# One-core attention and SOLU mixture kernel: W2 products two groups side by side, and float16 passes for half of the value products

## The chip, the cores and the metric

The kernel runs on one core of one Trainium2 chip. The metric is the device time of one execution in microseconds (us), lower is better. TensorE multiplies matrices (PE in the profile; its weight loads are listed apart as PEld), VectorE is DVE, ScalarE is ACT, GpSimd is POOL and SyncE, which issues the transfers, is SP.

## The reference: what is computed

Batch 4, 8 heads, 576 positions, head dimension 64: block-causal attention (blocks of 64), then four dense layers on the 2304 tokens.

```
scores = scale * q @ k.T ; masked where block_i < block_j
attn   = exp(scores - max) / (sum + 1e-9)
x      = attn @ v                       # 2304 x 512
a, b   = x @ w1, x @ w2                 # 2304 x 1024
h      = (a * b) @ w3 @ w_out           # 2304 x 512
h2     = h @ w_in                       # 2304 x 1024
solu   = h2 * softmax(h2)
out    = layernorm(solu) * g_ln @ w_out2   # 2304 x 512
```

The inputs are float64 or float32 as the reference makes them; the kernel folds w3 @ w_out into one 1024 x 512 matrix, W2, on the chip.

## The kernel before, in words

The kernel is written as many small generators, one for each piece of work (a load, a score block, a product of a token group). Each yields its instructions one at a time with the buffers that they read and write and a cost in ns. A planner, `Program.run` (from line 130), keeps a clock for each engine and always emits the instruction that could start first; between several it takes the one with the lower order number. Those numbers are given at `M.spawn` (lines 1144 to 1201) out of the constants of line 282: `PB` and `BS` for batches 2 and 3, `MB`, `MS` and `FS` for token groups, `YO`, `HO`, `OO` for the three later steps of a group, `AO`, `RO`, `VO` for the steps of attention. So a change of costs, buffers or constants changes the order of the instructions on every engine's queue.

**Attention** goes by batch and pair of heads (16 pairs). `scores` (L481) makes q k.T of two heads in two halves of the array's rows; `row_max` (L499), `expo` (L505), `norm`; `flip` (L651) transposes the probabilities on PE into PSUM and copies them to the tiles `ta` (first 320 positions, part 0) and `tb` (last 256, part 1). `values` (L699) multiplies by v in float32: the two heads of a pair write the upper and lower 64 partitions of one PSUM bank, so a pair needs three chunks of positions for part 0 (320, 192 and 64 columns) and five for part 1 (256, 256, 256, 192, 64). In the trace each float32 matmul is two records. The result is scaled (L730) and split into a high and a low float16 part, `xs`, a ring of five token groups.

**Token groups** are nine groups of 256 tokens. `u_ab` (L960) makes a and b for one of 8 column blocks f, in three float16 passes (high by high, high by low, low by high; 24 matmuls of 256 columns), multiplies them into `asb` and splits that into high and low, `ghl`. `u_y` (L1005) multiplies with W2: 8 f x 4 blocks x 3 passes = 96 matmuls of 256 columns for each group. `u_h` (L1049) multiplies with w_in for each half of 128 tokens: 24 matmuls of 512 columns, followed by the softmax and layer norm chain on DVE and ACT and eight transposes (L1097). `u_out` (L1128) makes 24 float16 matmuls of 512 columns and the output transfer.

```
for e in range(NE):
    for q, (s, t) in enumerate(((0, 0), (0, 1), (1, 0))):
        yield op("PE", 123.0, lambda: pe.matmul(
            ps[:, e // 2, e % 2 * N : (e % 2 + 1) * N],
            lhsT=W2s[:, f, s, e * P : (e + 1) * P], rhs=hl[:, t, :], ...
```

The matrices are streamed in, decoded on DVE and split during the first third of the time. When the last value product has been issued (`after_attention`, line 1215), memory is given to further `ghl`, `asb`, `t`, `uT` and `osb` buffers; four PSUM banks become a second `yh` and two `ab`.

Of the kernel before, what the change touches and what calls it, by code (L numbers as in the profile page):

```python
# [7 lines left out]
F16 = mybir.dt.float16  # L8
# [9 lines left out]
P = 128  # L18
# [196 lines left out]
def block_attention_moe_solu(ctx: ExitStack, tc: tile.TileContext, qk0, qk, vr, w1, w2, w3r, wout, win, wout2, gln, out):  # L215
# [54 lines left out]
    def acq(tag):  # L270
        return ("acq", tag)
# [7 lines left out]

    done = M.done  # L280
    ENG = "APd"
    PS, PO, OG, OA, PD, DS, P1, PG, PW, W2P, AS, PA, PB, BS, MB, MS, FS, YO, HO, OO, AO, RO, VO, DT, P0, K0, W2S, A1, V0, PX, OB, NL = 1009.16, 770.75, 0, 1, -202.05, 1099.57, -2137.11, 346.55, -822.9, -836.48, -602.44, 345.86, 8206.72, 1129.12, -34.34, 7256.56, 225.91, 1732.11, -202.54, -41.89, -10.2, -22.05, -93.34, 228.46, 105.76, 24, 6518, 216.01, 1896.05, 127.52, 0, -92.74
    M.DETOUR = DT


# [25 lines left out]
    negs = const.tile([64, 64], F32, name="negs")  # L311
# [3 lines left out]
    ring(const, "bc", 1, [P, P], F32)  # L315
    ring(const, "sm", 4, [P, 28], F32)
# [6 lines left out]
    apool = ctx.enter_context(tc.tile_pool(name="apool", bufs=1))  # L323
# [12 lines left out]
    mpool = ctx.enter_context(tc.tile_pool(name="mpool", bufs=1))  # L336
    ring(mpool, "asb", 2, [P, N], F32)
    ring(mpool, "ghl", 3, [P, 2, N], F32R)
    ring(mpool, "y", 1, [P, 2, NE, N], F32R)
    vstack = ExitStack()  # L340
# [27 lines left out]
    def pow2_scale(i, name, m, mk):  # L368

        t = scl[:, i]  # L370
        k = ("scl", i)
        ib = yield acq("bc")
        bc, kb = T["bc"][ib], ("bc", ib)
# [5 lines left out]
        rel("bc", ib)  # L379
# [111 lines left out]
    def mask(t, k):  # L491
        return ways(
            [], [k], ("DVE", SMALL, lambda: dve.memset(t, NEG)),
            ("ACT", c_act(64), lambda: act.copy(t, negs)),  # L494
        )

    def row_max(t, dst, k, kd):
# [88 lines left out]
    def norm(b, h, part):  # L586
# [36 lines left out]

    BANKS = ((("e01", (0, 1)), ("e2", (2,))), (("e3", (3,)), ("e4", (4,)), ("e4", (5,))))
    HELD = {0: ("pa", 0, 1), 1: ("pa", P, 2), 2: ("pd", 0, 3), 3: ("pb", 0, 4), 4: ("pc", 0, 4), 5: ("pc", 4 * P, 1)}

    def flip(b, h, part, n):

# [14 lines left out]
        for x in tiles:  # L643
            tag, c0, nb = HELD[x]
            ip = X[b, h, tag]
            p = T[tag][ip]
            kp = [(tag, ip, z) for z in ((4, 5) if x == 4 else (x,))]
            for c in range(nb):
                yield op(
                    "PE", c_mr(P),  # L650
                    lambda: pe.transpose(t[:, o + c * P : o + (c + 1) * P], p[:, c0 + c * P : c0 + (c + 1) * P], ident),  # L651
                    kp, [k],
                )
            if x == 0:
                outs.append((64, t[:, o : o + 64], pt[:, 0, 0:64]))
            elif x == 5:
                outs.append((64, t[:, o + 64 : o + P], pt[:, 4, 192:256]))
            else:
                q = {1: 64, 2: 192, 3: 0, 4: P}[x]
                src = t[:, o : o + nb * P].rearrange("p (a n) -> p a n", n=P)  # L660
                outs.append((nb * P, src, pt[:, 0:nb, q : q + P]))
            o += nb * P
        for tag in sorted({HELD[x][0] for x in tiles}):
            m = X[b, h, tag, "n"] = X.get((b, h, tag, "n"), 0) + 1
            if m == (2 if tag == "pc" else 1):
                rel(tag, X.pop((b, h, tag)))
        for w, src, dst in outs:
            yield ways([], [k, (ptag, ipt, n)], *copies(w, dst, src, 1.0, "Ad"))
# [8 lines left out]
    def values(b, hp, part):  # L677
# [11 lines left out]
        iv = X[b, hp, "vv"]  # L689
        vv = T["vraw"][iv]  # L690
        i = yield acq("ab")
        t, k = T["ab"][i], ("ab", i)
        for q, (c, o) in enumerate(REACH[part]):

            kr = slice(0, D if c == NT - 1 else P)

            def both():
                for j in range(2):
                    pe.matmul(  # L699
                        t[j * D : (j + 1) * D, o:w], lhsT=vv[kr, c, j], rhs=T[ptag][ipt[j]][kr, c, o:w],  # L700
                        start=(q == 0), stop=(q == len(REACH[part]) - 1),
                    )

            yield op(
                "PE", 4 * (w - o) / 2.4 + 80, both,
                [(ptag, x, n) for x in ipt for n in range(len(BANKS[part]))] + [("vraw", iv), (("vraw", iv), "z")], [k],
            )
        for j in range(2):
            rel(ptag, ipt[j])
        nv = X[b, hp, "nv"] = X.get((b, hp, "nv"), 0) + 1  # L710
        if nv == 2:
            rel("vraw", iv)
        for j in range(2):
            yield ev(("r", b, 2 * hp + j, part))
        ir = X.pop((b, hp, part, "rb"))
# [223 lines left out]
    def u_ab(g, f):  # L939
# [8 lines left out]
        ih = yield acq("ghl")  # L948
        a = yield acq("ab")
        done(("ab", g, f))  # L950
        ps, k = T["ab"][a], ("ab", a)
# [18 lines left out]
                    q += 1  # L970
        ia = yield acq("asb")
        asb, ka = T["asb"][ia], ("asb", ia)
        hl, kh = T["ghl"][ih], ("ghl", ih)
# [13 lines left out]
        X["ghl", g, f] = ih  # L987
        done(("g", g, f))

    def u_y(g):  # L990
# [36 lines left out]
        rel("yh", i)  # L1027
        X["y", g] = iy
        done(("y", g))

    def u_h(g, i):
        yield ev("lpool")
# [111 lines left out]
    def attention(b, hp, p):  # L1144
        M.spawn(p, load_qk(b, hp))
        M.spawn(p, prep_qk(b, hp))
        M.spawn(p + V0, load_v(b, hp))
        M.spawn(p + AO, s_01(b, hp))
        M.spawn(p + 2 * AO, s_23(b, hp, 2))
        M.spawn(p + 3 * AO, s_23(b, hp, 3))  # L1150
# [43 lines left out]
    for g in range(NG):  # L1194
        p = MB + MS * g
        for f in range(NF):
            M.spawn(p + FS * f, u_ab(g, f))
        M.spawn(p + YO, u_y(g))
# [15 lines left out]
    def after_attention():  # L1214

        M.retire("ab", range(2, 6))
        vstack.close()
        gpool = ctx.enter_context(tc.tile_pool(name="gpool", bufs=1, reuse_waits="tile"))
        more("ghl", *[gpool.tile([P, 2, N], F32R, name=f"ghl{3 + i}") for i in range(3)])
        for tag in ("pa", "pd"):  # L1220
            more("asb", *[t[:, 0:N] for t in T[tag]])
        more("t", T["qk"][0][:, 0:1024].rearrange("p (a c) -> p a c", a=2))
        for t in T["tb"]:
            more("uT", t.bitcast(F16).rearrange("p c n -> p (c n)")[:, 0 : 2 * DFF].rearrange("p (z f n) -> p z f n", z=2, f=NF))
        more("osb", T["vraw"][0].rearrange("p c h d -> p (c h d)")[:, 0:512])

    def after_banks():
        astack.close()
# [59 lines left out]
```

## Time and profile before

| | |
|---|---|
| time, median of 3 runs | 784.7 us (783.59 to 787.49) |
| the profiled execution: its own time | 782.93 us |
| the profiled execution: span of its instructions | 781.2 us |
| granted TensorE clock, mean | 0.998 |
| PE busy | 751.9 us (96%) |
| DVE busy | 443.6 us (57%) |
| ACT busy | 356.2 us (46%) |

A row of the chain of waits gives a start, a length, and what ran: `634.71 8.64 PE yh L1005 x72` is 72 records of line 1005 from 634.71 us on, 8.64 us in all. A row of the windows gives a stretch, its length, and each engine's busy time with its count of instructions. A row of the groups gives busy time and the mean duration of one in ns; matmuls overlap, so the mean is longer than the step from one to the next.

### The profile page before, as it was taken

The numbers are of one execution on the slowest core, as the hardware profiler recorded it, in microseconds if no ns is written. First come the engines' busy times: TensorE is split into PE (matmuls) and PEld (weight loads), VectorE is DVE, ScalarE is ACT, GpSimd is POOL, SyncE is SP. The second block draws the span as 40 slices with busy tenths as digits, with TensorE's granted clock in tenths as the row PEclk, the third lists the DMA queues.
The fourth block names the chain that finished last, engine by engine and source line by source line (L and its number), as shares of the span: only waits on it lengthen the run. The fifth ranks groups of instructions, "written<-read, shape, count | busy, mean of one in ns | idle before, by whom it ended". The sixth has DMA issues, their size and how long they took to land.

```text
span 781.2 us, 13588 instructions
## 1 busy us (share of the span) xinstructions
PE 751.9 (96%) x5193; PEld 557.0 (71%) x5193; DVE 443.6 (57%) x1191; ACT 356.2 (46%) x1008; POOL 192.2 (25%) x277
## 2 busy tenths in 40 slices
PE   6799998999899999999999999999999999999998
PEld 3445444777575887678767877688798698698974
DVE  7898998999974156455474338323504416216243
ACT  4657745677744344566166545441322322213222
POOL 1213324678821102222032112120210111112100
PEclk9999999999999999999999999999999999999999
DMA  7666665554122100313101110000000000000001
GB/s 222 210 223 197 215 231 179 163 163 151 45 72 70 39 1 15 91 32 111 27 15 44 32 31 1 28 1 1 14 14 1 14 16 1 28 1 1 1 1 55
DMA packets 36545, 53.84 MB, mean 69 GB/s; under 512 B 22272, under 2 KB 24576, under 8 KB 36480
## 3 DMA queue, kind: packets, MB, share of 16 engines
q1 hardware_dynamic: 36480, 52.97, 21.6%
q8 instruction: 41, 0.67, 0.4%
q14 instruction: 24, 0.20, 0.1%
HBM read 48.24 MB, written 4.72 MB: 68 GB/s over the span
## 4 chain that ended last, share of the span: by engine, by line
PE 86%; DVE 10%; ACT 1%; POOL 1%; issue 1%; DMA 1%; SPq 0%; ACTq 0%; DVEq 0%; POOLq 0%
PE ab L960 23%; PE yh L1049 13%; PE yh L1005 12%; PE ab L1128 12%; PE ab L481 7%; PE ab L651 6%; PE ab L880 5%; PE ab L699 5%; PE ab L1097 2%; DVE st L499 1%; PE ab L722 1%; DVE w3f L774 1%; DVE w3f L782 1%; DVE w3f L778 1%; DMA qk<-in_qk_dram 1%
## 5 line engine op out<-in xcount | busy, mean ns | idle before, releaser
L1005 PE MATMUL yh<-ghl,W2s 128*128 128x256 f32 x864 | 119.9, 289 | 1.4 <-POOL ghl L262 1.4
L960 PE MATMUL ab<-xs,w2s 128*128 128x256 f16 x864 | 114.6, 273 | 0.0
L960 PE MATMUL ab<-xs,w1s 128*128 128x256 f16 x864 | 111.5, 275 | 0.1
L1005 PEld LDWEIGHTS yh<-ghl,W2s 128*128 128x128 f32 x864 | 107.7, 189 | 4.5 <-issue 2.4
L1049 PE MATMUL yh<-winHL,y 128*128 128x512 f32 x432 | 102.1, 393 | 0.0
L960 PEld LDWEIGHTS <-w2s 128*128 128x128 f16 x864 | 83.6, 98 | 14.0 <-issue 4.0
L1049 PEld LDWEIGHTS yh<-winHL,y 128*128 128x128 f32 x432 | 80.1, 188 | 17.3 <-issue 0.4
L960 PEld LDWEIGHTS <-w1s 128*128 128x128 f16 x864 | 81.9, 98 | 14.4 <-issue 3.5
L499 DVE TENSOR_REDUCE st<-ab 128x1 f32<-128x288 f32 (+4 forms) x192 | 75.5, 411 | 1.3 <-ACT ab L494 0.3
L481 PE MATMUL ab<-qk 64*128 64x288 f32 (+4 forms) x384 | 68.8, 434 | 7.2 <-POOL qk L255 6.3
L1128 PE MATMUL ab<-gWs,uT 128*128 128x512 f16 x336 | 75.7, 379 | 0.0
L262 POOL TENSOR_TENSOR ghl<-asb,ghl 128x256 fp32r<-128x256 f32 x48 | 38.2, 796 | 115.8 <-ACT ghl L252 101.6
L880 PE MATMUL ab<-woutF,w3f 128*128 128x512 f32 x128 | 61.2, 604 | 2.9 <-DVE woutF L782 2.6
L1128 PEld LDWEIGHTS <-uT 128*128 128x128 f16 x336 | 32.5, 98 | 36.3 <-issue 0.4
L481 PEld LDWEIGHTS ab<-qk 64*128 64x128 f32 (+1 forms) x384 | 32.2, 180 | 32.2 <-issue 8.7
L979 DVE SCALAR_TENSOR_TENSOR asb<-ab,dsc,asb 128x256 f32<-128x256 f32 (+3 forms) x66 | 25.6, 397 | 49.3 <-ACT asb L252 49.0
L1067 DVE TENSOR_REDUCE sm<-yh 128x1 f32<-128x1024 f32 x18 | 22.0, 1224 | 46.2 <-PE yh L1049 46.2
L505 ACT ACTIVATE pc<-ab,st 128x288 f32<-128x288 f32 x64 | 31.9, 503 | 32.8 <-DVE st L569 31.6
L255 POOL TENSOR_SCALAR rb<-st,scl 128x128 f32<-128x128 f32 (+1 forms) x50 | 23.3, 469 | 90.1 <-PE ab L722 31.3
L252 ACT ACTIVATE asb<-ab,dsc 128x256 f32<-128x256 f32 (+3 forms) x58 | 22.6, 413 | 40.5 <-PE ab L960 39.9
L262 POOL TENSOR_TENSOR xs<-rs,xs 128x256 f16<-128x256 f32 (+3 forms) x36 | 26.5, 736 | 58.4 <-ACT xs L252 55.1
L880 PEld LDWEIGHTS ab<-woutF,w3f 128*128 128x128 f32 x128 | 21.9, 190 | 25.2 <-issue 19.0
(160 smaller groups left out, 1154.5 us busy)
## 6 DMA issues: line engine op xcount, KB each, us to landing
qk<-in_qk_dram SPq DMA_DIRECT2D x16, 576.0 KB, 4.2
raw<-in_w3r_dram SPq DMA_DIRECT2D x16, 512.0 KB, 4.6
raw<-in_wout_dram SPq DMA_DIRECT2D x16, 512.0 KB, 3.8
raw<-in_w_dram SPq DMA_DIRECT2D x16, 512.0 KB, 4.5
raw<-in_win_dram SPq DMA_DIRECT2D x8, 512.0 KB, 3.7
vraw<-in_vr_dram SPq DMA_DIRECT2D x18, 192.0 KB, 2.4
out_dram<-osb SPq DMA_DIRECT2D x13, 256.0 KB, 2.0
vraw<-in_vr_dram SPq DMA_DIRECT2D x32, 80.0 KB, 3.4
```

The costliest lines, as they stand in the source:

```text
L262: "P": ("POOL", c_tt(n, dst.dtype), lambda: pool.tensor_tensor(dst, a, b, op=ALU.subtract)),
L481: pe.matmul(dst, lhsT=t[h, q0 : q0 + rows], rhs=t[h, k0 + c0 : k0 + c0 + cols], start=True, stop=True)
L499: "DVE", c_dve(t.shape[-1]), lambda: dve.tensor_reduce(dst, t, axis=AX.X, op=ALU.max, negate=True), [], [k, kd]
L505: lambda: act.activation(p, t, AF.Exp, bias=nm, accum_out=sm), [ks], [k, kp, (ks, "s")],
L651: lambda: pe.transpose(t[:, o + c * P : o + (c + 1) * P], p[:, c0 + c * P : c0 + (c + 1) * P], ident),
L699: pe.matmul(t[j * D : (j + 1) * D, o:w], lhsT=vv[kr, c, j], rhs=T[ptag][ipt[j]][kr, c, o:w], start=(q == 0), stop=(q == len(REACH[part]) - 1),
L880: lambda: pe.matmul(ps, lhsT=t[:, jc, :], rhs=woutF[:, jc, :], start=(jc == 0), stop=(jc == NF - 1)),
L960: lambda: pe.matmul(ps[:, n * N : (n + 1) * N], lhsT=w[:, x * NE + hp, s, fs], rhs=xs[:, hp, t, x0 : x0 + N], start=(q == 0), stop=(q == 3 ...
L979: lambda: dve.scalar_tensor_tensor(asb[:, c0:c1], ps[:, N + c0 : N + c1], dsc[:, b, x, 1:2], asb[:, c0:c1], op0=ALU.mult, op1=ALU.mult), [ ...
L1005: lambda: pe.matmul(ps[:, e // 2, e % 2 * N : (e % 2 + 1) * N], lhsT=W2s[:, f, s, e * P : (e + 1) * P], rhs=hl[:, t, :], start=(f == 0 and ...
L1049: lambda: pe.matmul(ps[:, n, :], lhsT=y[:, a, e, ts], rhs=X["win"][e // 2][:, e % 2, b, n * 512 : (n + 1) * 512], start=(e == 0 and (a, b) ...
L1128: lambda: pe.matmul(ps, lhsT=uT[:, s, f, :], rhs=gWs[:, f, t, :], start=(q == 0), stop=(q == 3 * NF - 1)),
```

## The change

1. Groups 5 and 6, and 7 and 8, are paired (`PAIR`). `u_ab` of both writes its high and low parts into the two halves of a common tile `gp` (eight of them, one for each f, 512 columns), and `u_y2` replaces `u_y` for them: 48 matmuls of 512 columns for each half of the output, 96 for a pair of groups. Groups 0 to 4 stay.
2. For batches 2 and 3 `values` uses three float16 passes instead of float32. `flip` writes a high and a low float16 part, scaled by 2^13, in the room of the float32 tile; `split_v` does the same for v into a new tile `vhl` (one buffer); the scale in `norm` follows.
3. Buffers: the attention tiles and the value tiles are given back together once attention is done, and `gp` (8), one more `y`, one more `t`, one more `uT` take their room; the extra `ghl`, `asb`, `osb` buffers go; `bc` goes (its user takes an `asb`); `negs` is one column.
4. Other constants in line 282.

```diff
-PB, BS, MB, MS, FS, YO, HO, OO, AO, RO, VO = 8206.72, 1129.12, -34.34, 7256.56, 225.91, 1732.11, -202.54, -41.89, -10.2, -22.05, -93.34
+PB, BS, MB, MS, FS, YO, HO, OO, AO, RO, VO = 7906.4, 765.4, -723.76, 7510.2, 186.21, 5034.19, -135.9, -413.38, -1.27, 244.18, -1116.8
...
+    ring(const, "vhl", 1, [P, 2, NT, 2, D], F16)
...
+    def split_v(b, hp):
...
+            yield ways([kv, (kv, "z"), ks], [(k, x)], *copies(n, hi, src, s[rows], "Ad"))
+            yield op("DVE", c_dve(n) + 62,
+                lambda: dve.scalar_tensor_tensor(lo, src, s[rows], hi, op0=ALU.mult, op1=ALU.subtract), ...
     def flip(b, h, part, n):
...
+            if b < NAT:
+                yield ways([], [k, (ptag, ipt, n)], *copies(w, dst(pt), src, 1.0, "Ad"))
+                continue
+            hi, lo = (dst(pt[:, z]) for z in range(2))
+            yield ways([k], [(ptag, ipt, n)], *copies(w, hi, src, PSC, "Ad"))
+            yield op("DVE", c_dve(w) + 62,
+                lambda: dve.scalar_tensor_tensor(lo, src, PSC, hi, op0=ALU.mult, op1=ALU.subtract), ...
     def values(b, hp, part):
...
+            for m, (x, y) in enumerate(((0, 0), (0, 1), (1, 0))):
+                yield op("PE", max((w - o) / 2.4 + 10, 60.0),
+                    lambda: both(lambda v: v[:, x], lambda p: split_view(p)[:, y], q == 0 and m == 0, q == end and m == 2), kk, [k])
...
     def u_ab(g, f):
...
+            if g == PAIR[g]:
+                ih = X["gp", g, f] = yield acq("gp")
+                done(("gp", g, f))
+            else:
+                yield ev(("gp", g - 1, f))
+                ih = X["gp", g - 1, f]
+            z = g - PAIR[g]
+            hl, kh = T["gp"][ih][:, :, z * N : (z + 1) * N], ("gp", ih, z)
...
+    def u_y2(g):
+        yield ev(("hps", g - 1, 1))
+        for x in range(2):
+            i = yield acq("yh")
+            ps, k = T["yh"][i], ("yh", i)
+            for f in range(NF):
...
+                for n in range(2):
+                    e = 2 * x + n
+                    for q, (s, t) in enumerate(((0, 0), (0, 1), (1, 0))):
+                        yield op("PE", 230.0, lambda: pe.matmul(ps[:, n, :],
+                            lhsT=W2s[:, f, s, e * P : (e + 1) * P], rhs=T["gp"][ih][:, t, :], ...
...
+            if x == 0:
+                iy = yield acqs("y", 2)
+            for z in range(2):
...
     def after_attention():
...
-        more("ghl", *[gpool.tile([P, 2, N], F32R, name=f"ghl{3 + i}") for i in range(3)])
-        for tag in ("pa", "pd"):
-            more("asb", *[t[:, 0:N] for t in T[tag]])
...
+        for tag, n, shape, dt in (("gp", 8, [P, 2, 2 * N], F32R), ("y", 1, [P, 2, NE, N], F32R), ("t", 1, [P, 2, 512], F32), ("uT", 1, [P, 2, NF, P], F16)):
+            more(tag, *[gpool.tile(shape, dt, name=f"{tag}{len(T[tag]) + x}") for x in range(n)])
```

## Rows read from the trace of the kernel before

**Rows 1.** The page's first part: busy time and share of each engine.
```profile
PE 751.9 (96%) x5193; PEld 557.0 (71%) x5193; DVE 443.6 (57%) x1191; ACT 356.2 (46%) x1008; POOL 192.2 (25%) x277
```

**Rows 2.** Windows: stretch and length; busy PE, PEld, DVE, ACT, POOL; clock, DMA share, GB/s.
```profile
0.00:240.00 240.00, 214.34 (x1278) 135.52 (x1279) 213.76 (x535) 153.16 (x440) 103.54 (x130) 0.99 0.53 169
240.00:514.00 274.00, 274.00 (x2046) 206.80 (x2044) 134.45 (x446) 135.69 (x426) 53.68 (x99) 1.00 0.13 38
514.00:757.00 243.00, 243.00 (x1772) 204.55 (x1771) 85.33 (x185) 61.09 (x132) 33.61 (x48) 1.00 0.02 8
757.00:781.20 24.20, 20.54 (x103) 10.12 (x102) 10.10 (x27) 6.29 (x10) 1.38 (x2) 1.00 0.12 44
```

**Rows 3.** Chain of waits, group 6 from its W2 products to w_in: start, us, what.
```profile
626.57 1.43 PE yh L1005 x12
...
630.63 1.45 PE yh L1005 x12
632.08 2.63 PE ab L960 x24
634.71 8.64 PE yh L1005 x72
...
645.77 10.91 PE yh L1049 x48
```

**Rows 4.** Chain of waits, one value product of part 0 and one of part 1.
```profile
467.05 1.13 PE ab L699 x12
...
512.13 2.03 PE ab L699 x20
```

**Rows 5.** Windows of line 699 alone, 240 to 514 us: PE, PEld busy.
```profile
240.00:514.00 274.00, 28.57 (x276) 17.36 (x276) 1.00 0.13 38
```

**Rows 6.** Groups by form, weight loads of value products and of `u_ab`.
```profile
L960 PEld LDWEIGHTS <-w2s 128*128 128x128 f16 x864 | 83.6, 98 | 14.0 <-issue 4.0
...
L699 PEld LDWEIGHTS ab<-tb,vraw 128*64 128x64 f32 x256 | 16.8, 136 | 13.4 <-issue 2.3 <-DVE tb L254 1.4 <-ACT rs L252 0.8
```

**Rows 7.** Groups by form on DVE, 240 to 514 us.
```profile
L1102 DVE TENSOR_TENSOR uT<-ab,uT 128x512 f16<-128x512 f32 x14 | 9.5, 681 | 5.8 <-ACT uT L252 5.8
...
L979 DVE SCALAR_TENSOR_TENSOR asb<-ab,dsc,asb 128x256 f32<-128x256 f32 x13 | 6.2, 476 | 22.9 <-ACT asb L252 22.8
...
L979 DVE SCALAR_TENSOR_TENSOR asb<-ab,dsc,asb 128x128 f32<-128x128 f32 x8 | 2.7, 338 | 0.1
...
L979 DVE SCALAR_TENSOR_TENSOR asb<-ab,dsc,asb 128x64 f32<-128x64 f32 x8 | 2.1, 265 | 4.2 <-ACT asb L252 4.2
```

**Rows 8.** Windows of 40 us, columns as in rows 2.
```profile
120.00:160.00 40.00, 35.13 (x269) 25.96 (x267) 38.76 (x78) 27.24 (x56) 25.69 (x21) 0.96 0.52 165
160.00:200.00 40.00, 36.95 (x308) 30.37 (x307) 38.56 (x85) 29.47 (x80) 30.70 (x31) 1.00 0.45 149
200.00:240.00 40.00, 36.73 (x227) 26.00 (x226) 33.55 (x87) 25.54 (x80) 18.84 (x29) 1.00 0.17 52
...
280.00:320.00 40.00, 40.00 (x260) 28.65 (x258) 25.62 (x85) 18.67 (x62) 7.03 (x13) 1.00 0.07 23
```

**Rows 9.** Chain of waits at the end, group 8 and the last outputs.
```profile
746.51 10.92 PE yh L1049 x48
757.43 5.20 PE ab L1128 x24
...
770.20 7.35 PE ab L1128 x34
```

**Rows 10.** Timeline, DVE steps of the first half of group 8.
```profile
752.03 1.23 DVE L1067 TENSOR_REDUCE sm<-yh 128x1 f32<-128x1024 f32 x1 [5.48 <-PE yh L1049]
...
754.52 1.22 DVE L1069 TENSOR_TENSOR qk<-qk,yh 128x1024 f32<-128x1024 f32 x1 [1.27 <-ACT qk L1068]
755.78 1.29 DVE L1072 BATCH_NORM_STATS2 sm<-qk 128x6 f32<-128x512 f32 x2
...
761.10 0.81 DVE L1087 TENSOR_SCALAR qk<-qk,sm 128x1024 f32<-128x1024 f32 x1
...
763.72 0.69 DVE L1102 TENSOR_TENSOR uT<-ab,uT 128x512 f16<-128x512 f32 x1 [0.56 <-ACT uT L252]
```

More of the change, by code (lines that the diff above doesn't have):

```diff
@@ L234, in block_attention_moe_solu @@
     HC = 512
+    PAIR = [None if g < R else g - (g - R) % 2 for g in range(NG)]
     M = Program()
@@ L321, in block_attention_moe_solu @@
     T["tmp"] = M.add_slots("tmp", [tmp16[:, i] for i in range(NE)])
-    apool = ctx.enter_context(tc.tile_pool(name="apool", bufs=1))
+    mpool = ctx.enter_context(tc.tile_pool(name="mpool", bufs=1))
+    ring(mpool, "asb", 2, [P, N], F32)
+    ring(mpool, "ghl", 3, [P, 2, N], F32R)
+    ring(mpool, "y", 1, [P, 2, NE, N], F32R)
+    vstack = ExitStack()
+    apool = vstack.enter_context(tc.tile_pool(name="apool", bufs=1))
     for tag, n, shape, dt in (
@@ L334, in block_attention_moe_solu @@
         ring(apool, tag, n, shape, dt)
[L336 to L340, printed above, removed]
+    T["gp"] = M.add_slots("gp", [])
     vpool = vstack.enter_context(tc.tile_pool(name="vpool", bufs=1))
@@ L371, in pow2_scale @@
         k = ("scl", i)
-        ib = yield acq("bc")
-        bc, kb = T["bc"][ib], ("bc", ib)
+        ib = yield acq("asb")
+        bc, kb = T["asb"][ib][:, 0:P], ("asb", ib)
         yield ways([mk], [kb], *copies(P, bc, m.to_broadcast([P, P]), 1.0, "PA"))
@@ L378, in pow2_scale @@
         yield op("PE", c_mr(P), lambda: pe.transpose(pt[:, 0:P], bc, ident), [kb], [ka])
-        rel("bc", ib)
+        rel("asb", ib)
         yield op("DVE", c_dve(P), lambda: dve.tensor_reduce(t[:, 0:1], pt[:, 0:P], axis=AX.X, op=ALU.max), [], [ka, k])
@@ L493, in mask @@
             [], [k], ("DVE", SMALL, lambda: dve.memset(t, NEG)),
-            ("ACT", c_act(64), lambda: act.copy(t, negs)),
+            ("ACT", c_act(64), lambda: act.copy(t, negs.to_broadcast([64, 64]))),
         )
@@ L625, in block_attention_moe_solu, with split_view @@
     HELD = {0: ("pa", 0, 1), 1: ("pa", P, 2), 2: ("pd", 0, 3), 3: ("pb", 0, 4), 4: ("pc", 0, 4), 5: ("pc", 4 * P, 1)}
+    PSC = 2.0 ** 13
+    def split_view(t):
+        c = t.shape[1]
+        return t.rearrange("p c n -> p (c n)").bitcast(F16).rearrange("p (z c n) -> p z c n", z=2, c=c)
+    def split_v(b, hp):
+        yield ev(("vv", b, hp))
+        yield ev(("scale", ("v", b)))
+        s, _, ks = SC["v", b]
+        iv = X[b, hp, "vv"]
+        vv, kv = T["vraw"][iv], ("vraw", iv)
+        i = yield acq("vhl")
+        t, k = T["vhl"][i], ("vhl", i)
+        for x, (rows, cs) in enumerate(((slice(0, P), slice(0, NT - 1)), (slice(0, D), slice(NT - 1, NT)))):
+            n = (cs.stop - cs.start) * 2 * D
+            src = vv[rows, cs]
+            hi, lo = (t[rows, z, cs] for z in range(2))
+            yield ways([kv, (kv, "z"), ks], [(k, x)], *copies(n, hi, src, s[rows], "Ad"))
+            yield op(
+                "DVE", c_dve(n) + 62,
+                lambda: dve.scalar_tensor_tensor(lo, src, s[rows], hi, op0=ALU.mult, op1=ALU.subtract),
+                [kv, (kv, "z"), ks], [(k, x)],
+            )
+        rel("vraw", iv)
+        X[b, hp, "vhl"] = i
+        done(("vhl", b, hp))
     def flip(b, h, part, n):
@@ L667, in flip @@
         for w, src, dst in outs:
-            yield ways([], [k, (ptag, ipt, n)], *copies(w, dst, src, 1.0, "Ad"))
+            if b < NAT:
[3 more added lines that the diff above has]
+            yield ways([k], [(ptag, ipt, n)], *copies(w, hi, src, PSC, "Ad"))
+            yield op(
+                "DVE", c_dve(w) + 62,
+                lambda: dve.scalar_tensor_tensor(lo, src, PSC, hi, op0=ALU.mult, op1=ALU.subtract), [k], [(ptag, ipt, n)],
+            )
         rel("ab", i)
@@ L688, in values @@
                 yield ev(("g", g - R, f))
-        iv = X[b, hp, "vv"]
-        vv = T["vraw"][iv]
+        split = b >= NAT
+        if split:
+            yield ev(("vhl", b, hp))
+        vtag = "vhl" if split else "vraw"
+        iv = X[b, hp, "vhl" if split else "vv"]
+        vv = T[vtag][iv]
+        kv = [("vraw", iv), (("vraw", iv), "z")] if not split else [(("vhl", iv), x) for x in range(2)]
         i = yield acq("ab")
@@ L695, in values, with both @@
             kr = slice(0, D if c == NT - 1 else P)
-            def both():
+            def both(va, pa, first, last):
                 for j in range(2):
                     pe.matmul(
-                        t[j * D : (j + 1) * D, o:w], lhsT=vv[kr, c, j], rhs=T[ptag][ipt[j]][kr, c, o:w],
-                        start=(q == 0), stop=(q == len(REACH[part]) - 1),
-                    )
[L704 to L707, printed above, removed]
+                        t[j * D : (j + 1) * D, o:w], lhsT=va(vv)[kr, c, j], rhs=pa(T[ptag][ipt[j]])[kr, c, o:w], start=first, stop=last
+                    )
+            end = len(REACH[part]) - 1
+            kk = [(ptag, x, n) for x in ipt for n in range(len(BANKS[part]))] + kv
+            if not split:
+                yield op("PE", 4 * (w - o) / 2.4 + 80, lambda: both(lambda v: v, lambda p: p, q == 0, q == end), kk, [k])
+                continue
+            for m, (x, y) in enumerate(((0, 0), (0, 1), (1, 0))):
+                yield op(
+                    "PE", max((w - o) / 2.4 + 10, 60.0),
+                    lambda: both(lambda v: v[:, x], lambda p: split_view(p)[:, y], q == 0 and m == 0, q == end and m == 2), kk, [k],
+                )
         for j in range(2):
@@ L711, in values @@
         if nv == 2:
-            rel("vraw", iv)
+            rel(vtag, iv)
         for j in range(2):
@@ L947, in u_ab @@
             yield ev(("ab", g - (f == 0), (f - 1) % NF))
[L948 removed]
+        if PAIR[g] is None:
+            ih = yield acq("ghl")
+            hl, kh = T["ghl"][ih], ("ghl", ih)
+        else:
+            if g == PAIR[g]:
+                ih = X["gp", g, f] = yield acq("gp")
+                done(("gp", g, f))
+            else:
+                yield ev(("gp", g - 1, f))
+                ih = X["gp", g - 1, f]
+            z = g - PAIR[g]
+            hl, kh = T["gp"][ih][:, :, z * N : (z + 1) * N], ("gp", ih, z)
         a = yield acq("ab")
@@ L986, in u_ab @@
         rel("asb", ia)
-        X["ghl", g, f] = ih
+        if PAIR[g] is None:
+            X["ghl", g, f] = ih
         done(("g", g, f))
@@ L1029, in u_y @@
         done(("y", g))
+    def u_y2(g):
[5 more added lines that the diff above has]
+                for z in range(2):
+                    yield ev(("g", g + z, f))
+                yield ev(("W2", f))
+                ih = X["gp", g, f]
+                for n in range(2):
+                    e = 2 * x + n
+                    for q, (s, t) in enumerate(((0, 0), (0, 1), (1, 0))):
+                        yield op(
+                            "PE", 230.0,
+                            lambda: pe.matmul(
+                                ps[:, n, :],
+                                lhsT=W2s[:, f, s, e * P : (e + 1) * P],
+                                rhs=T["gp"][ih][:, t, :],
+                                start=(f == 0 and q == 0),
+                                stop=(f == NF - 1 and q == 2),
+                            ), [("gp", ih, 0), ("gp", ih, 1), ("W2", f)], [k],
+                        )
+                if x == 1:
+                    rel("gp", X.pop(("gp", g, f)))
+            if x == 0:
+                iy = yield acqs("y", 2)
+            for z in range(2):
+                v = ps[:, :, z * N : (z + 1) * N]
+                d = [T["y"][iy[z]][:, a, 2 * x : 2 * x + 2, :] for a in range(2)]
+                yield ways([k], [("y", iy[z], x)], *copies(512, d[0], v, 1.0, "Ad"))
+                yield op(
+                    "DVE", c_dve(512), lambda: dve.tensor_tensor(d[1], v, d[0].bitcast(F32), op=ALU.subtract),
+                    [k], [("y", iy[z], x)],
+                )
+            rel("yh", i)
+        for z in range(2):
+            X["y", g + z] = iy[z]
+            done(("y", g + z))
     def u_h(g, i):
@@ L1147, in attention @@
         M.spawn(p + V0, load_v(b, hp))
+        if b >= NAT:
+            M.spawn(p + V0 + 1, split_v(b, hp))
         M.spawn(p + AO, s_01(b, hp))
@@ L1197, in block_attention_moe_solu @@
             M.spawn(p + FS * f, u_ab(g, f))
-        M.spawn(p + YO, u_y(g))
+        if PAIR[g] is None:
+            M.spawn(p + YO, u_y(g))
+        elif PAIR[g] < g:
+            M.spawn(p + YO, u_y2(g - 1))
         for i in range(2):
```

22 lines of the change are left out of this document (8 added, 14 removed).

## The prediction, made before the changed kernel ran

> **What bounds the kernel now.** I began with the page's first part [rows 1]: PE is busy for 96% of the span, and no other engine comes near. As busy shares are means over stages, I then took the windows by stage [rows 2]. The reader is to see two regimes. Before 240 us PE is busy for 214.34 of 240 us while DVE is at 213.76: weights are decoded and the first two batches are under way, and PE misses 25.7 us. From 240 us to the end of the chain PE is busy for every microsecond (274.00 of 274, 243.00 of 243), while DVE is at half load or less. There, time goes down by exactly what is taken out of PE's own stream, and work added to DVE or ACT is free so long as it is not late. The chain of waits gives the price of PE's pieces as steps, not as overlapping durations: [rows 3] for the W2 and w_in products, [rows 4] for the value products. The chain at the end [rows 9] shows PE without a hole as well: 757.43 us plus its pieces leads to 777.55 us, and what follows is one copy and the output transfer.
>
> **The change, part by part.** Durations come from the profiled execution, 782.93 us (span 781.2 and 1.7 around it); it lies 1.8 us, 0.2%, under the median of 784.7. The sum is a difference and is taken off the median.
>
> *W2 products in pairs.* Removed: 4 groups x 96 matmuls of 256 columns. One group costs 1.43 + 1.45 + 8.64 = 11.52 us [rows 3], 120 ns a matmul, so 46.1 us. Added: 192 matmuls of 512 columns in the same float32r format. Line 1049 has that very form: 48 take 10.91 us [rows 3], 227 ns each, so 43.6 us. Gain 2.4 us: joining two products saves no columns, only the excess of the 256-column step over half of the 512-column one. Bounds: at the float16 step (5.20 us for 24 [rows 9], 217 ns) the gain is 4.5 us; with 230 ns, as where other work is mixed in, 2 us.
>
> *Value products of batches 2 and 3.* Eight pairs of heads. A part 0 costs 1.13 us, a part 1 2.03 us [rows 4], 25.3 us for the eight, which agrees with the 28.57 us of line 699 after 240 us [rows 5], as that includes overlap and 20 records of batch 1. By columns: part 0 has 320 + 192 + 64 = 576 per head, part 1 1024. The step of [rows 9] gives 0.423 ns a column. Four passes of 576 and 1024 columns make 0.975 and 1.73 us; so the two heads of a pair run side by side in the array (one after the other they would need twice this, more than was measured), and 0.155 and 0.30 us are entry, short chunks and the change of array shape. Three passes make 0.73 and 1.30 us. If the overhead stays, a pair of heads saves 0.24 + 0.43 us, 5.4 us for eight. If it grows with the records (18 for 12, 30 for 20) the saving is 0.17 + 0.285, 3.6 us for eight. I take 5.4: the array changes its shape once per product, not once per pass.
>
> The last chunk has 64 columns, and there the load of the weights may set the pass. Loads are shown for float16 with 128 columns at 98 ns and for float32 with 64 at 136 ns [rows 6]; a float16 load of 64 columns is not shown. If a pass of that chunk takes half of a 110 ns step (2.63 us for 24 with 128-column loads [rows 3]), 55 ns where the columns alone would need 27, the six short passes of a pair cost 0.17 us more, 1.3 us for eight, which lies inside the two bounds. The Trainium skill, TensorEngine Tiling (Array Packing), Gotcha 2, says that column tiling excludes the fast weight load, so float16 would bring the loads of these half-width products nothing; by that rule 4.1 us are saved here and not 5.4.
>
> *Added evacuation.* Each `flip` copy gets a second DVE step: per head 64, 256, 384, 512, 512 and 64 columns. With 265, 476, 580 (between its neighbours), 681, 681 and 265 ns [rows 7] this is 2.95 us a head, 47.2 us for 16 heads; `split_v` adds 681 + 338 ns eight times, 8.2 us. So 55 us of DVE, and some 7 us of ACT. They lie in 240 to 514 us, where DVE has 134.45 of 274 us in use [rows 2]: 190 of 274 afterwards, 69%. I cost this at nothing; the cover is PE's token group work. If the cover is gone, see the first rival. In `flip` the low part waits for the high part and keeps the PSUM bank some 0.7 us longer; queued behind it on DVE are row maxima, on PE the next scores, which have other banks. `split_v` waits for the one `vhl` buffer, so for the second part of the previous pair's product; some 34 us pass between pairs (274 / 8), its own work takes 2 us.
>
> *Buffers.* `asb` goes from six to two after attention. One is held for four steps, of which the DVE step takes 0.48 us [rows 7], and PE needs 2 x 2.63 us [rows 3] to fill two, so none is waited for. `osb` goes to one, with an output every 5.2 us [rows 9]. Both at nothing; bounds are nothing as well, since PE would have other pieces ready. DMAs are neither added nor moved past another's queue by design; their order can shift with the constants.
>
> *The end.* Group 7's halves now come directly ahead of group 8's. A half costs PE 5.45 us [rows 3] and DVE 1.23 + 1.22 + 1.29 + 0.81 + 2 x 0.69 and small steps, some 7 us [rows 10]. Four halves in a row put DVE some 6 to 8 us behind, and four outputs of 5.2 us stand ready to cover that. No gain either, as PE had no hole there.
>
> *Order numbers.* They can only matter where PE waits, in the first 240 us, or if they make a new wait. The trace shows no price for them. Nearest row: at equal DVE load PE got 35.13 us in one window and 36.95 in the next [rows 8], 1.8 us apart; over the three windows from 120 to 240 us, where group work and attention compete, that bounds the effect at 5.5 us either way. I take zero, as no row favours a sign.
>
> Sum: 2.4 + 5.4 = 7.8 us; 784.7 - 7.8 = **776.9 us**.
>
> **The rivals.**
>
> *DVE takes PE's place in batches 2 and 3 (slower).* The new constants put batch 3's last pair at 770.75 + 2 x 7906.4 + 6 x 765.4 = 21,176 (23,959 before), ahead of group 3 at about 21,807 (21,735 before), so attention comes denser just as it needs 55 us more of DVE. What it looks like is seen from 120 to 200 us: DVE at 38.8 and 38.6 of 40, PE at 35.1 and 36.95 [rows 8], 4 us lost in 40. If all 190 us of DVE work ran in that state, 196 us or 4.9 windows would lose 19.4 us: 796. Against it: with DVE at 25.62 of 40 PE lost nothing [rows 8]. It decides once over three windows are saturated (7.8 plus the 3.9 us of the measurement's limit). The Trainium skill, TensorEngine Tiling, PSUM Bottleneck, warns that after a TensorE speedup the copy out of PSUM may become the bound; by that rule the result is this rival's 796, and the trace's 69% speaks against it.
>
> *The start of the order changes.* With the same work, the first 240 us lose or gain 5.5 us: 771.4 or 782.4. For a gain: 25.7 us of holes lie there [rows 2]. For a loss: DVE, at 89%, has no slack there, and value products are moved ahead of other work by over 1000 in order number.
>
> *PE runs out of cover near 514 us.* Group 5 can't start before attention has ended, as `gp` exists only then. Before, some of group 4 was left at that point. If it is used up, PE waits for the last heads' chain, at most some 10 us: 787. I count it with the losses of order.
>
> *The float16 passes don't run side by side.* Then three passes of both heads cost 1.70 and 3.05 us with overhead: 1.58 us more per pair instead of less, 12.6 us, and 794.9 in all. Only float32 pairs are seen side by side [rows 4].
>
> **How the numbers follow.** The forecast as it stands, from 774 to 780: 0.52. Order gains, near 771: 0.20. Order loses or cover runs out, 782 to 787: 0.16. DVE-bound, 789 to 796: 0.09. Serial passes, 795: 0.03. About 0.5%, 3.9 us, is what a measurement here can tell from no change: faster is below 780.8, slower above 788.6. Faster: 0.52 + 0.20 = 0.72. Same: 0.16. Slower: 0.12. The range goes from both gains at their upper bounds with the order's gain (784.7 - 4.5 - 5.4 - 5.5 = 769.3) to both at their lower with its loss (784.7 - 2.0 - 3.6 + 5.5 = 784.6): 769 to 784, which leaves out about 0.15 to 0.2.
>
> **What would show it.** W2 products of groups 5 to 8: 192 records of 512 columns, 227 ns apart. Value products of batches 2 and 3: 18 and 30 records, near 0.89 and 1.60 us. PE still fully busy from 240 us to its end; DVE near 190 us in that stretch of attention, under 34 of 40 in each window. The forecast is wrong if PE shows holes after 240 us, if value products take over 1.13 and 2.03 us, or if the first regime ends several us earlier or later with the same work done.

## The result and the profile after

The changed kernel takes 773.49 us (772.19 to 773.86, 4 runs) against 784.14 us for the kernel before in the same runs: ratio 0.9861, 95% interval 0.9844 to 0.9878. That is 10.7 us less; 7.8 had been forecast (776.9 us), and the range of 769 to 784 holds the result. The profiled execution took 773.70 us, its span 771.9 us.

The page's first part, which answers to [rows 1]:

```profile
PE 746.6 (97%) x5129; PEld 551.3 (71%) x5129; DVE 475.9 (62%) x1279; ACT 368.6 (48%) x1043; POOL 193.7 (25%) x282
```

PE has 64 instructions less: 192 fewer W2 products, 128 more records of value products. DVE has 32 us more.

The windows by stage, columns as in [rows 2]:

```profile
0.00:240.00 240.00, 218.55 (x1292) 140.08 (x1293) 212.47 (x543) 156.39 (x452) 103.95 (x128) 0.98 0.55 171
240.00:514.00 274.00, 273.98 (x2234) 214.48 (x2233) 170.32 (x531) 146.78 (x454) 56.09 (x108) 1.00 0.13 36
514.00:757.00 243.00, 242.82 (x1553) 191.33 (x1551) 90.31 (x201) 62.29 (x132) 32.92 (x46) 1.00 0.02 9
757.00:771.90 14.90, 11.28 (x57) 5.42 (x54) 2.78 (x7) 3.12 (x5) 0.69 (x1) 1.00 0.14 53
```

The two regimes are still there. After 240 us PE is as full as before although DVE does 36 us more in the middle stretch (170.32 for 134.45). Before 240 us PE is busy for 4.2 us more than in [rows 2], at a DVE load that hardly differs: holes were closed there that the forecast had left as they were. But not all of the 4.2 us is work done. The first 120 us, of the kernel before and of the changed one:

```profile
0.00:120.00 120.00, 105.52 (x478) 53.19 (x479) 102.89 (x288) 70.92 (x226) 28.32 (x51) 1.00 0.69 217
0.00:120.00 120.00, 108.04 (x478) 55.78 (x479) 104.80 (x301) 67.79 (x217) 31.65 (x53) 0.97 0.69 219
```

In the changed kernel the granted clock falls to its lower level (1.2 GHz) for part of the stretch from 30 to 40 us (mean 0.71), after PE was busy for 6.74 of the 10 us before; in the kernel before it stays at 1.00 there. A mean of 0.97 for 1.00 over 120 us is some 3.6 us of full clock, by my estimate, so by that estimate most of the 4.2 us went into the slower clock.

The chain of waits, for one float16 value product of part 0 (18 records) and one of part 1 (30), and for the two paired W2 products:

```profile
251.40 0.87 PE ab L746 x18
...
284.60 1.56 PE ab L746 x30
...
588.93 22.39 PE yh L1110 x96
...
699.39 22.40 PE yh L1110 x96
```

Against 1.13 and 2.03 us [rows 4], a pair of heads saves 0.26 + 0.47 = 0.73 us, eight pairs 5.8 us; 0.89 and 1.60 us had been forecast. The paired W2 products take 44.8 us, 233 ns for each matmul of 512 columns, where 227 had been assumed.

At the end the chain shows the four halves of groups 7 and 8 in a row, and it now passes through DVE before it returns to PE:

```profile
725.87 10.20 PE yh L1153 x45
...
739.71 1.14 DVE sm L1171
...
746.88 1.59 POOL sm L1188 x2
...
751.86 8.63 PE ab L1232 x40
...
762.45 5.84 PE ab L1232 x27
```

DVE is the later one there, as the forecast's section on the end had it, but outputs fill PE: it is busy for 242.82 of 243 us up to 757 us. PE's last piece ends at 768.29 us, 3.6 us ahead of the span's end; before it was 777.55, again 3.6 to 3.7 us. The end gave and cost nothing.

### The profile page after: what moved, and what is told of

It is laid out like the page before. It is cut to its first block, busy times and chain, and to the rows that moved or that the text cites. A ratio compares the mean times of both kernels' runs of the same rounds, so it can differ in the third digit from the quotient of the medians.

```text
span 771.9 us, 13594 instructions
## 1 busy us (share of the span) xinstructions
PE 746.6 (97%) x5129; PEld 551.3 (71%) x5129; DVE 475.9 (62%) x1279; ACT 368.6 (48%) x1043; POOL 193.7 (25%) x282
## 4 chain that ended last, share of the span: by engine, by line
PE 82%; DVE 12%; ACT 3%; POOL 1%; issue 1%; DMA 1%; SPq 0%; DVEq 0%; ACTq 0%
PE ab L1023 22%; PE yh L1153 12%; PE ab L1232 11%; PE yh L1068 6%; PE ab L484 6%; PE yh L1110 6%; PE ab L685 6%; PE ab L932 5%; PE ab L746 4%; PE ab L1201 2%; DVE st L502 2%; PE ab L774 1%; DVE w3f L834 1%; DVE w3f L826 1%; DVE w3f L830 1%
## 5 line engine op out<-in xcount | busy, mean ns | idle before, releaser
L1232 PE MATMUL ab<-gWs,uT 128*128 128x512 f16 x432 | 97.4, 379 | 0.0
L1041 DVE SCALAR_TENSOR_TENSOR asb<-ab,dsc,asb 128x256 f32<-128x256 f32 (+3 forms) x96 | 37.9, 409 | 89.7 <-ACT asb L254 89.4
L1023 PEld LDWEIGHTS <-w2s 128*128 128x128 f16 x864 | 84.1, 98 | 12.4 <-issue 2.2
L502 DVE TENSOR_REDUCE st<-ab 64x1 f32<-64x64 f32 (+4 forms) x192 | 75.5, 411 | 2.3 <-ACT ab L497 1.6
L1232 PEld LDWEIGHTS <-uT 128*128 128x128 f16 x432 | 41.7, 98 | 46.9 <-issue 1.1
L1068 PE MATMUL yh<-ghl,W2s 128*128 128x256 f32 x480 | 73.7, 293 | 0.0
L1068 PEld LDWEIGHTS yh<-ghl,W2s 128*128 128x128 f32 x480 | 61.3, 189 | 6.6 <-issue 6.1
L254 ACT ACTIVATE asb<-ab,dsc 128x256 f32<-128x256 f32 (+3 forms) x86 | 34.5, 419 | 53.4 <-PE ab L1023 46.4
L264 POOL TENSOR_TENSOR gp<-asb,gp 128x256 fp32r<-128x256 f32 x32 | 23.4, 732 | 102.1 <-ACT gp L254 90.7
L1110 PE MATMUL yh<-gp,W2s 128*128 128x512 f32 x192 | 45.3, 396 | 0.0
L1110 PEld LDWEIGHTS yh<-gp,W2s 128*128 128x128 f32 x192 | 35.8, 188 | 8.6
```

Source lines behind the costliest of these rows:

```text
L254: "A": ("ACT", c_act(n, 0 if num else 1, 0, "D" in engines), (lambda: act.copy(dst, src)) if num and s == 1.0 else (lambda: act.activation ...
L264: "P": ("POOL", c_tt(n, dst.dtype), lambda: pool.tensor_tensor(dst, a, b, op=ALU.subtract)),
L502: "DVE", c_dve(t.shape[-1]), lambda: dve.tensor_reduce(dst, t, axis=AX.X, op=ALU.max, negate=True), [], [k, kd]
L1023: lambda: pe.matmul(ps[:, n * N : (n + 1) * N], lhsT=w[:, x * NE + hp, s, fs], rhs=xs[:, hp, t, x0 : x0 + N], start=(q == 0), stop=(q == 3 ...
L1041: lambda: dve.scalar_tensor_tensor(asb[:, c0:c1], ps[:, N + c0 : N + c1], dsc[:, b, x, 1:2], asb[:, c0:c1], op0=ALU.mult, op1=ALU.mult), [ ...
L1068: lambda: pe.matmul(ps[:, e // 2, e % 2 * N : (e % 2 + 1) * N], lhsT=W2s[:, f, s, e * P : (e + 1) * P], rhs=hl[:, t, :], start=(f == 0 and ...
```

## The experiments

Twelve kernels ran, each also timed against the kernel before on the same chip (medians of 783.75 to 784.23 us there). Differences are taken between medians; with ratios whose 95% interval is about 0.0015 to either side, a difference between two kernels is good to 1 or 2 us. Almost every edit also lets the planner choose another order, so a difference holds the effect of that too. The first four kernels take the change apart; the diffs are shortened, with `...` where a line goes on.

**Value products back in float32.** The splitting starts at batch 4, so nowhere.

`NAT` gives way to `VSP` in `flip`, `norm` and the spawn of `split_v` as well.

```diff
+    VSP = 4
...
-        split = b >= NAT
+        split = b >= VSP
```

> The changed kernel with the value products of batches 2 and 3 back in float32 (no split of v, no second DVE step in flip); pairs, buffers and constants as changed. Theory PE (after 240 us the time follows PE's own steps; the value products give 0.26 + 0.47 us a pair of heads): 773.5 + 5.9 = 779.4 us, DVE busy down by about 45 us without any gain from it. Rival order (the constants made most of the 10.7 us): 773 to 775 us. Rival DVE (the 45 us of added DVE work cost something): below 777 us.

Measured 778.84 us, ratio 0.9936 [0.9924, 0.9949]: 5.3 us above the changed kernel. The windows of 240 to 514 us:

```profile
240.00:514.00 274.00, 274.00 (x2059) 209.14 (x2057) 132.28 (x450) 136.68 (x414) 53.71 (x95) 1.00 0.12 36
```

DVE loses 38 us of work there and nothing is gained by it, while the time rises by 5.3 us (5.9 by the ratios) where the chain says 5.8. Theory PE holds; no cost of the added DVE work can be told from the noise.

**W2 products one group at a time.**

```diff
-    PAIR = [None if g < R else g - (g - R) % 2 for g in range(NG)]
+    PAIR = [None] * NG
...
-        ("gp", 8, [P, 2, 2 * N], F32R)
+        ("ghl", 3, [P, 2, N], F32R)
```

> The changed kernel with the W2 products of groups 5 to 8 again one group at a time (256 columns, three more high/low buffers instead of the eight common ones). Theory PE: 384 matmuls at 120 ns for 192 at 233 ns, 773.5 + 1.3 = 774.8 us, at most 775.9 (the 2.4 us of the prediction). Rival order: anything from 770 to 780, since the planner's order changes with the buffers.

Measured 773.70 us, ratio 0.9872 [0.9859, 0.9885]: 0.2 us, no difference that can be told. Its chain shows why, for one group, in the same three pieces as [rows 3]:

```profile
562.11 1.40 PE yh L1068 x12
...
566.15 1.41 PE yh L1068 x12
...
570.19 8.40 PE yh L1068 x72
```

The 256-column matmul, 120 ns in the kernel before, takes 117 ns here (8.40 / 72), which is half of the 233 ns of the paired one. Four groups cost 4 x 11.21 = 44.8 us, to the tenth what the pairs cost and 1.3 us less than the 46.1 us of the kernel before. So this 1.3 us comes with or without pairs; joining two saves nothing. The price goes with the columns, and its excess over the 0.423 ns a column of the float16 step [rows 9] differs from place to place (8% here, 11% in the kernel before, 5% on line 1153). Why is not shown.

**The constants of before in the changed kernel, and the new ones in the kernel before.**

The first of the two edits, with only the eleven constants of the line; the second is its reverse.

```diff
-PB, BS, MB, MS, FS, YO, HO, OO, AO, RO, VO = 7906.4, 765.4, -723.76, ...
+PB, BS, MB, MS, FS, YO, HO, OO, AO, RO, VO = 8206.72, 1129.12, -34.34, ...
```

> The changed kernel with the constants of the kernel before. Theory PE: the parts keep 5.9 + 1.3 us, the 2 to 3 us that the trace shows in the first 240 us go: 775.5 to 777 us, with PE still full after 240 us. Rival order: 780 us or more.

> The kernel before with the changed constants alone. Theory PE: 781 to 782.5 us (784.1 less the 2 to 3 us of the first 240 us). Rival order: 776 us or less.

Measured 778.82 us for the first (ratio 0.9943 [0.9928, 0.9957]) and 783.10 us for the second (0.9991 [0.9980, 1.0001]). Both expectations missed. In the changed kernel the constants are worth 5.3 us, twice what I had read from the trace; alone, in the kernel before, 0.65 us by the medians (783.75 to 783.10), and the interval includes no change. The first stretch of the one with the old constants looks like that of the kernel before [rows 2]; the second line is the kernel before with the new ones:

```profile
0.00:240.00 240.00, 213.97 (x1278) 135.40 (x1279) 214.06 (x535) 153.09 (x440) 103.78 (x129) 0.99 0.55 169
0.00:240.00 240.00, 219.17 (x1288) 140.64 (x1289) 210.20 (x535) 154.04 (x447) 104.81 (x131) 0.98 0.53 167
```

The new constants close 4.6 us of holes in the one kernel (218.55 less 213.97) and 4.8 in the other (219.17 less 214.34), both at a lower mean clock, and yet the time gains 5.3 us in the one and next to nothing in the other. So the holes of the first stretch do not carry the 5.3 us by themselves, and what does is open. By the medians the three removals add up, 5.3 + 0.2 + 5.3 = 10.8 of the 10.7 us, but with noise of 1 or 2 us in each that closeness says little (the ratios give 5.9, 0.9 and 6.4 us), and the constants are no term of their own, as they give 0.65 us without the rest.

**Which constants.** Two further kernels put back three (AO, RO, VO, the steps of attention) and two (PB, BS, the place of batches 2 and 3).

```diff
-AO, RO, VO = -1.27, 244.18, -1116.8
+AO, RO, VO = -10.2, -22.05, -93.34
```

> The changed kernel with three constants of before, those of the steps of attention (AO, RO, VO). All eleven of before cost 5.3 us. Theory start (the gain of the constants lies in the first 240 us, through the order of attention's steps of batches 0 and 1): 776.5 to 779 us, PE busy in the first 240 us down by 3 to 5 us, full from there on. Rival (the gain lies after 240 us, in how dense batches 2 and 3 are): 773.5 to 774.5 us.

```diff
-PB, BS = 7906.4, 765.4
+PB, BS = 8206.72, 1129.12
```

> The changed kernel with the two constants of before that place batches 2 and 3 (PB, BS). Theory start: 773 to 774.5 us, the first 240 us as in the changed kernel. Rival (their place is what matters, as cover for the last heads): 777 us or more, with PE's waits near the end of attention.

Measured 782.51 us (0.9973 [0.9960, 0.9987]) and 775.67 us (0.9893 [0.9878, 0.9909]). The three alone cost 9.0 us, more than all eleven together; the two cost 2.2 us, near the noise. Neither expectation held: the effects lie on both sides of 240 us. The windows of 0 to 240 and 240 to 470 us, for the kernel with the three constants put back:

```profile
0.00:240.00 240.00, 216.00 (x1269) 137.89 (x1270) 214.22 (x530) 149.02 (x426) 102.52 (x124) 0.98 0.54 169
240.00:470.00 230.00, 228.04 (x1815) 176.84 (x1814) 139.17 (x440) 120.62 (x368) 43.42 (x83) 1.00 0.15 42
```

Besides the first stretch, PE loses 2 us after 240 us, where neither the kernel before nor the changed one has a hole. There it is not steps of attention that wait: the view of PE's waits from 240 to 514 us has 1.1 us of W2 products (line 1068) behind DVE's L1173 and 0.7 us of a group's transposes (line 1201) behind L1206. With PB and BS of before PE has 1.7 us of holes from 240 to 514 us, and 1.1 us of waits there (0.6 on line 1201, 0.5 on line 1023) end with L709, the new second step of `flip`. The rest of the 9.0 us, and which single order does it, was not followed further.

**DVE's second step made twice** in the flips of batches 2 and 3, then for one of the batches alone.

```diff
             yield op("DVE", c_dve(w) + 62,
                 lambda: dve.scalar_tensor_tensor(lo, src, PSC, hi, op0=ALU.mult, op1=ALU.subtract), ...
+            yield op("DVE", c_dve(w) + 62,
+                lambda: dve.scalar_tensor_tensor(lo, src, PSC, hi, op0=ALU.mult, op1=ALU.subtract), ...
```

> The changed kernel with the second DVE step of every flip of batches 2 and 3 made twice, 96 instructions and about 45 us more on DVE between 240 and 514 us; results are unchanged. Theory PE (DVE work there is covered): 773.5 to 775.5 us, PE full after 240 us, DVE some 215 of 274 us. Rival DVE (the stretch is near DVE's bound): 781 us or more, with PE waiting for DVE in the value products or transposes.

Measured 786.02 us, ratio 1.0037 [1.0023, 1.0050]: 12.5 us more, and slower than the kernel before, for 33 us more on DVE by the page's first part:

```profile
PE 755.1 (96%) x5129; PEld 553.0 (70%) x5129; DVE 508.9 (65%) x1375; ACT 372.3 (47%) x1046; POOL 193.1 (25%) x279
```

My expectation failed, and the rival's time (781 us or more) came. Windows of 40 us, columns as in [rows 8], show the loss without a DVE that looks full:

```profile
360.00:400.00 40.00, 38.38 (x291) 30.03 (x290) 31.28 (x96) 23.02 (x69) 8.19 (x17) 1.00 0.16 45
...
440.00:480.00 40.00, 38.91 (x323) 29.45 (x320) 31.68 (x88) 24.31 (x75) 6.43 (x12) 1.00 0.08 23
480.00:520.00 40.00, 36.91 (x251) 25.92 (x251) 27.43 (x88) 19.62 (x60) 9.40 (x19) 0.87 0.02 8
```

A narrower window at the last heads, 476 to 500 us, shows it, first of the changed kernel:

```profile
476.00:500.00 24.00, 24.00 (x179) 16.00 (x179) 16.89 (x65) 12.42 (x40) 4.46 (x9) 1.00 0.05 19
```

and of the one with the doubled step:

```profile
476.00:500.00 24.00, 19.82 (x139) 14.42 (x138) 21.25 (x73) 12.15 (x39) 5.38 (x11) 0.79 0.00 1
```

DVE is at 21.25 of 24 us here, PE at 19.82, and the granted clock is down to a mean of 0.79 after PE's idle time, so that part of the 19.82 is slow. That is 4.2 us of idle time and, by an estimate from the mean (0.21 of 24 us), up to 5.0 us of full clock. The timeline of PE in that place, and one step of DVE:

```profile
490.48 0.55 PE L685 MATMUL ab<-ident,pd 128*128 128x128 f32 x3
492.16 0.77 PE L685 MATMUL ab<-ident,pc 128*128 128x128 f32 x5 [1.14 <-DVE tb L713]
492.76 0.60 PE L1205 MATMUL ab<-ident,t 128*128 128x128 f32 x4
494.96 2.29 PE L1027 MATMUL ab<-xs,w1s 128*128 128x256 f16 x10 [1.59 <-DVE tb L713]
...
491.42 0.81 DVE L713 SCALAR_TENSOR_TENSOR tb<-ab,tb 128x512 f16<-128x512 f32 x2
```

Both long waits end with a second low part (L713). What waits the second time is not attention: line 1027 is the product of a token group, it reads neither `ta` nor `tb`, and all that it shares with L713 is the PSUM tile `ab`, which L713 reads. So group work was next on PE, and what it lacked, by the releaser that the trace gives, was a free bank. How far waits like this depend on the place is what the two kernels test that double one batch alone, `b == 2` in the first and `b == 3` in the second:

```diff
+            if b == 2:
+                yield op("DVE", c_dve(w) + 62, ...
```

> The second DVE step of flip made twice for batch 2 alone (about 23 us more DVE). Doubling it for both batches took 12.5 us, with no window of DVE over 32 of 40 us and most of PE's waits between 476 and 500 us, at the last heads. Theory cover (what counts is whether PE still has token group work when DVE is late; batch 2 has it): at most 2 us more, 773.5 to 775.5 us. Rival DVE share (each us of DVE costs the same): half of 12.5 us, 779 to 780.5 us.

> The same for batch 3 alone. Theory cover (the last heads have nothing left behind them): 9 us or more, 782 to 786 us, with PE's waits between 470 and 510 us. Rival DVE share: 779 to 780.5 us, waits spread over the stretch.

Measured 777.40 us (0.9916 [0.9903, 0.9930]) for batch 2 and 782.97 us (0.9987 [0.9978, 0.9996]) for batch 3: 3.9 and 9.5 us for nearly the same added work (17 and 16 us of DVE by their pages, 493.2 and 492.1 us). Windows of 240 to 470 and 470 to 510 us, first for batch 2:

```profile
240.00:470.00 230.00, 227.84 (x1815) 176.60 (x1813) 152.67 (x470) 117.96 (x356) 45.45 (x84) 1.00 0.14 40
470.00:510.00 40.00, 39.98 (x326) 29.56 (x323) 31.02 (x107) 25.68 (x83) 5.75 (x12) 1.00 0.04 15
```

then for batch 3:

```profile
240.00:470.00 230.00, 229.50 (x1854) 180.16 (x1852) 149.69 (x459) 125.03 (x385) 46.42 (x90) 1.00 0.14 41
470.00:510.00 40.00, 36.34 (x273) 27.04 (x273) 33.11 (x106) 21.72 (x67) 7.25 (x16) 0.87 0.02 8
```

Equal shares are ruled out, and the place matters: most of the loss lies at the last heads, as the theory of cover had it, and for batch 2 the 2 us that I had allowed were too little. Why it lies there is not shown to be a want of group work, by the wait of line 1027 above. How much of the 12.5, 3.9 and 9.5 us is the planner's new order and not DVE was not tested; three constants with no added work cost 9.0 us.

**Heads one after the other.** The same float16 matmuls, all of the first head and then all of the second.

```diff
-        for q, (c, o) in enumerate(REACH[part]):
+        for hd, q, (c, o) in [(hd, q, r) for hd in (((0,), (1,)) if split else ((0, 1),)) for q, r in enumerate(REACH[part])]:
...
-                for j in range(2):
+                for j in hd:
```

> The changed kernel with the float16 value products of a pair issued head after head instead of alternating, the same instructions in another order. Theory side by side (two heads share the array when they alternate): part 0 from 0.87 to about 1.5 us, part 1 from 1.56 to about 2.7 us, eight pairs 13 to 15 us more, 786 to 789 us. Rival (each matmul has the array to itself either way): no change, 773.5 us.

Measured 789.82 us, ratio 1.0079 [1.0065, 1.0093]: 16.3 us more, above the expected 13 to 15. The chain (a record of the shorter product belongs to the row before it):

```profile
282.01 3.11 PE ab L746 x30
...
339.64 1.47 PE ab L746 x17
```

1.56 us become 3.11 and 0.87 become 1.47. Two heads do share the array when they alternate in float16; the rival of serial passes falls. For float32 it stays what the prediction worked out from the columns.

**Float16 passes for batch 1 too** (VSP = 1 in the first experiment's diff).

> The changed kernel with float16 passes for batch 1 too, whose attention runs mostly before 240 us. PE saves 4 x 0.73 = 2.9 us, DVE gets about 27 us more where it is at 89%. Theory PE with cover (added DVE work is free only after 240 us): slower, 778 to 795 us, and the first stretch in which PE is always busy begins later. Rival (PE's steps decide everywhere): 770.6 us.

Measured 786.16 us, ratio 1.0026 [1.0012, 1.0040]: 12.7 us above the changed kernel. The window of 120 to 240 us, where batch 1 is, first of the changed kernel and then with the passes for batch 1:

```profile
120.00:240.00 120.00, 110.51 (x815) 84.30 (x814) 107.67 (x243) 88.60 (x236) 72.31 (x76) 0.99 0.41 123
120.00:240.00 120.00, 102.34 (x758) 78.96 (x757) 112.14 (x237) 78.97 (x190) 69.86 (x73) 0.89 0.36 114
```

PE is busy for 8.2 us less, and at a mean clock of 0.89, while DVE rises to 112.14 of 120 us. The same edit that gains where PE is full loses where DVE nearly is.

**Alternate banks in the paired products.**

```diff
-                for n in range(2):
-                    e = 2 * x + n
-                    for q, (s, t) in enumerate(((0, 0), (0, 1), (1, 0))):
+                for q, (s, t) in enumerate(((0, 0), (0, 1), (1, 0))):
+                    for n in range(2):
+                        e = 2 * x + n
```

> The changed kernel with the two inner loops of the paired W2 products exchanged, so that successive matmuls write alternate PSUM banks, as line 1153 does at 227 ns a matmul, instead of six in a row to one bank at 234 ns. Theory banks (the 7 ns are the price of writing one bank twice in a row): step 227 ns, 192 x 7 = 1.3 us, 772.2 us. Rival weights (line 1153 is faster because two matmuls in a row have the same weights, which these have less after the exchange): step 234 ns or more, 773.5 us or a little above.

Measured 773.16 us, ratio 0.9869 [0.9856, 0.9883], no difference. The chain:

```profile
588.21 22.39 PE yh L1110 x96
```

Again 233 ns a matmul. (By the loops above, three matmuls in a row write one bank in the changed kernel, not the six that I expected.) Alternating the banks gains nothing. The edit also changes which matmuls in a row have the same weights, so two effects that cancel are not excluded, and the weights were not varied by themselves. Of the twelve, none was measurably faster than the changed kernel.

## Why the prediction was right, and where its terms were off

*What bounds it.* Right for the changed kernel. After 240 us time follows PE's steps: removing the float16 passes cost 5.3 us with 38 us less on DVE.

*Value products.* 5.4 us forecast, 5.8 by the chain, 5.3 by removal. Of the two bounds the one that keeps the overhead per product was the right one. The Trainium skill, TensorEngine Tiling (Array Packing), Gotcha 2, excludes the fast weight load with column tiling. The trace agrees, as the loads of half the width are not shorter: the answer for the tile `vhl` has

```profile
L746 PEld LDWEIGHTS <-vhl x384: 102/110/113, 251.3 to 511.4; 128*64 128x64 f16 x168, 64*64 64x64 f16 x24
```

110 ns in the median (the middle of the three figures) for 64 columns, where float16 loads of 128 columns take 98 [rows 6]. But the 1.3 us that I had set on the loads of the short chunks did not appear, as the passes were no longer than forecast without it.

*W2 pairs.* 2.4 us forecast, 0.2 by removal, no difference: the step that failed is the one that took 120 and 227 ns from two different lines as prices of a width. In the changed kernel's own place, one group at a time costs 117 ns and a pair 233, the same for each column.

*Order numbers.* Zero forecast with 5.5 us either way, 5.3 us measured in the changed kernel. The sum came out near partly by luck, by two errors that offset each other in part: 2.2 us too much for the pairs, 5.3 too little for the order. No mechanism of the forecast gives the order's 5.3 us, and by which waits they come about is open. The forecast let order matter only in the first 240 us or by a new wait. New waits there are (with AO, RO and VO of before, PE loses 2 us after 240 us), but neither way accounts for the whole.

*DVE's cover.* Costed at nothing, and no cost can be told. The forecast put 55 us on DVE; the new steps keep it busy for 50.2 us (41.62 for L709 and 8.57 for L654, each by itself in the window of 240 to 514 us), but DVE's total rose by 32.3 us only. DVE makes fewer of the copies to `ta` and `tb` (33 for 44) and ACT rose by 12.4 us; the rest was not taken apart. The test that I had set for the rival was wrong: I had asked for windows of 40 us over 34 us, and the doubled step lost 12.5 us with none over 32 after 240 us. Most of that lay in 24 us at the last heads, where the longest wait of PE, 1.59 us, is one of group work for a PSUM bank that DVE was reading. The Trainium skill, TensorEngine Tiling (Array Packing), PSUM Bottleneck, warns that after a large speedup of TensorE the copy out of PSUM may become the bottleneck. The changed kernel does not show it (DVE at 16.89 of 24 us, PE full); the doubled one does at that place (21.25, PE at 19.82).

*Buffers and the end.* Both at nothing, and after 240 us no wait of PE for `asb` or `osb` is seen; whether the 1.3 us of the W2 products that came without the pairs is due to the other places of the buffers is not shown.

## What to carry to other kernels

Where one engine is full, take its steps from the chain in the very place that is edited; a price from another line can be off by more than the gain. Where a planner orders the work, a change of buffers or costs and the constants belong together: test them together, and don't add up their effects. Look for the cost of added work in a narrow window, at the end of a stage above all, and not in the mean share; ask there which buffer the added step holds, and who wants it.

## What the runs showed that was not expected

- float32r matmuls cost 0.443, 0.456 or 0.469 ns a column (227 for 512; 233 for 512 and 117 for 256; 120 for 256), depending on the line and the kernel and not on the width. The cause is open.
- Three of eleven constants, put back alone, cost 9.0 us; all eleven cost 5.3.
- The new constants close 4.6 to 4.8 us of PE's holes before 240 us in either kernel, but shorten only the changed one, and much of what they fill runs at a lower mean clock.
- A further 33 us of DVE work (by the page 508.9 us for 475.9), as much again as the change had added, were no longer free: 12.5 us, most of them from batch 3 (9.5 us alone).
